# The first gate's logits with stationary weights on four column groups

## The chip, the cores and the metric

The program runs on one core of one Trainium2 chip. Its time is the device time of one execution in microseconds (us), as a median of several runs. The core has five engines with instruction streams of their own: TensorE (PE in the profile, with its weight loads listed apart as PEld), VectorE (DVE), ScalarE (ACT), GpSimd (POOL) and SyncE (SP), which issues most of the transfers. An engine takes its instructions in the order written; engines wait for one another by semaphores.

## The reference, cut to what matters

The kernel computes an attention with a sliding window, then a mixture of experts with a capacity (here called the first one), then a second, dense mixture of experts. The change lies in the gate of the first mixture, whose input x has 1152 rows of 512 features:

```python
logits = x @ w_gate                          # (1152, 512) @ (512, 8)
expert_idx = np.argmax(logits, axis=1)
logits_s = logits - logits.max(-1, keepdims=True)
probs = np.exp(logits_s)
probs /= probs.sum(-1, keepdims=True) + 1e-09
gate_w = probs[np.arange(N), expert_idx]
...                                          # each expert takes its first 288 rows: relu(x w1) w2
out[i] = gate_w[i] * y[expert_idx[i], pos[i]]
```

All of it is computed in fp32, or in pairs of rounded parts that add up to fp32.

## The kernel before, in words

The attention and the first gate form the first stage, which ends some 108 us after the start. The sequence is cut into ten blocks of query rows: two batches of four blocks with 128 rows and one with 64 (block 4 and block 9). The eight heads are done in two groups of four, so there are twenty units; unit u belongs to block u // 2. For a unit the steps are `scores` (PE; operands on 64 partitions, two heads side by side on the two halves of the array's rows), `pick` and `limit` (DVE), `powers` (ACT), `turn_p` (PE transposes), `take_p` (the transposed powers into SBUF, on ACT, DVE and POOL), `values` (PE) and `norm` (DVE).

When both units of a block t are done, the gate follows: `turn_x.t` (four PE transposes), `take_x.t` (ACT copies them into `xT`), `logits.t` (PE), `top.t` (DVE finds the largest logit and its index), `gate.t` (ACT, the exponentials), `choice.t`, `count.t`, `place.t`, `mark.t`, `table.t`, `add_table.t` (DVE and PE, the row's place in its expert's list) and `scale_x.t` (the scaled row goes to DRAM).

The order of all steps is written out by hand in the string `ORDER`. A step name that stands there several times is a generator that goes on one piece at each place (`top.0` stands three times, for its three pieces). After each step the helper `in_order` ties every new instruction to the one before it on its engine, so each engine's stream is the order of that string. An engine does not skip an instruction that waits.

`logits` holds a 128x128 part of `xT` stationary and streams the gate's eight weight columns, repeated 15 times to 120 columns. There are four such matmuls, one for each 128 features, and they accumulate into one PSUM tile `lgp`. An fp32 matmul appears in the trace as two records, called passes here, so a block has eight. PSUM tiles with the tag "pt" come from one pool of four buffers: `lgp` and the transposes share it.

After the first stage come the eight experts of the first mixture (up to about 264 us), then the second mixture with PE busy nearly without a break to the end.

Of the kernel before, what the change touches and what calls it, by code (L numbers as in the profile page):

```python
# [33 lines left out]
rest_k.2 limit.2.0 turn_k.4 norm.0 take_k.4 limit.2.1 limit.2.1 powers.1.1 norm.0 turn_p.1.1 powers.2.0 scores.3
turn_p.2.0 rest_k.4 norm.0 turn_k.3 turn_q.3 pick.3.0 limit.3.0 limit.3.0 scores.4 load_v.1 powers.2.1 take_p.1.0
take_k.3 values.1.0 load_weight.1 pick.3.1 take_p.2.0 take_p.1.1 powers.3.0 limit.3.1 rest_k.3 turn_p.2.1 limit.3.1
split_hi.0 split_lo.0 split_hi.1 split_hi.2 values.1.1 split_hi.3 turn_q.4 pick.4.0 limit.4.0 split_lo.1 turn_p.3.0
split_lo.2 split_lo.3 limit.4.0 powers.4.0 norm.1 norm.1 scores.5 norm.1 take_p.2.1 pick.4.1 values.2.1 pick.5.1
take_p.3.0 load_weight.2 load_v.2 take_q.3 turn_x.0 limit.5.1 take_q.4 limit.4.1 rest_q.3 powers.3.1 load_block.5
take_x.0 values.2.0 load_weight.3 split_hi.4 limit.4.1 turn_p.3.1 norm.2 limit.5.1 split_lo.4 split_hi.5 pick.5.0  # L40
split_lo.5 norm.2 logits.0 split_hi.6 take_p.3.1 split_hi.7 turn_p.4.0 scores.6 top.0 norm.2 powers.5.1 limit.5.0
top.0 values.3.0 limit.5.0 pick.6.1 rest_q.4 take_p.4.0 split_hi.8 limit.6.1 pick.6.0 turn_p.5.1 values.3.1
limit.6.1 top.0 powers.4.1 norm.3 split_lo.6 turn_p.4.1 load_block.6 split_hi.9 split_hi.10 norm.3 scores.7
limit.6.0 split_hi.11 turn_k.5 norm.3 values.4.0 take_p.5.1 powers.5.0 turn_p.5.0 choice.0 pick.7.0 take_p.4.1
pick.7.1 limit.6.0 split_lo.7 values.4.1 limit.7.1 turn_q.5 gate.0 powers.6.1 take_p.5.0 turn_p.6.1 limit.7.1 norm.4
take_k.5 powers.6.0 take_q.5 scores.8 choice.0 norm.4 norm.4 turn_x.1 pick.8.0 take_p.6.1 limit.8.0 limit.7.0
limit.7.0 take_x.1 values.5.1 turn_p.6.0 load_v.3 values.5.0 turn_k.6 rows pick.8.1 limit.8.0 norm.5 logits.1
rest_k.5 take_k.6 top.1 count.0 norm.5 powers.7.0 take_p.6.0 norm.5 scores.9 pick.9.0 rest_k.6 powers.8.0 turn_x.2
# [3 lines left out]
powers.9.1 scale_x.0 turn_q.7 limit.10.1 powers.8.1 norm.6 choice.1 place.1 scores.11 top.2 norm.6 values.7.1  # L52
limit.11.0 take_p.7.0 powers.9.0 top.2 powers.10.0 take_q.7 turn_p.8.0 limit.11.1 limit.11.0 gate.2 load_block.9
rest_q.7 turn_p.8.1 turn_k.7 take_p.8.1 take_k.7 top.2 values.7.0 norm.7 norm.7 scale_x.1 load_v.8 take_p.8.0
turn_p.9.0 turn_p.9.1 norm.7 turn_p.10.0 take_p.9.0 scores.12 powers.10.1 turn_x.3 values.8.1 values.8.0 turn_p.10.1
choice.2 take_p.9.1 take_x.3 pick.12.1 logits.3 limit.12.1 rest_k.7 mark.0 norm.8 norm.8 limit.11.1 norm.8 count.2
take_p.10.0 pick.12.0 top.3 top.3 limit.12.1 limit.12.0 table.0 add_table.0 values.9.0 place.2 values.9.1
powers.11.1 take_p.10.1 norm.9 choice.2 limit.12.0 top.3 turn_p.11.1 powers.11.0 scores.13 take_p.11.1 norm.9 norm.9
values.10.0 load_block.8 turn_x.4 turn_p.11.0 mark.1 take_x.4 choice.2 choice.3 pick.13.0 gate.3 take_p.11.0
powers.12.1 values.10.1 load_v.6 pick.13.1 limit.13.0 table.1 logits.4 limit.13.0 norm.10 limit.13.1 count.3  # L60
add_table.1 scale_x.2 turn_k.8 norm.10 norm.10 turn_p.12.1 powers.12.0 split_lo.8 limit.13.1 values.11.1 turn_p.12.0
values.11.0 place.3 take_k.8 norm.11 turn_q.8 mark.2 scores.14 norm.11 top.4 norm.11 take_p.12.0 take_p.12.1
choice.3 powers.13.0 powers.13.1 rest_k.8 pick.14.0 top.4 limit.14.0 choice.3 gate.4 take_q.8 values.12.0 load_v.7
pick.14.1 table.2 limit.14.0 turn_p.13.1 top.4 values.12.1 mark.3 scale_x.3 powers.14.0 turn_q.9 rest_q.8 norm.12
turn_p.13.0 add_table.2 scores.15 norm.12 take_p.13.0 norm.12 take_p.13.1 turn_x.5 choice.4 take_x.5 values.13.0
turn_p.14.0 values.13.1 limit.14.1 take_q.9 limit.14.1 pick.15.0 pick.15.1 logits.5 rest_q.9 limit.15.1 limit.15.0
take_p.14.0 count.4 powers.14.1 table.3 turn_p.14.1 norm.13 limit.15.1 powers.15.1 top.5 norm.13 scores.16 choice.4
place.4 top.5 norm.13 take_p.14.1 limit.15.0 choice.3 gate.5 top.5 choice.4 pick.16.0 turn_p.15.1 scale_x.4
pick.16.1 take_p.15.1 values.14.1 turn_x.6 choice.5 limit.16.0 mark.4 values.14.0 load_v.9 turn_k.9 powers.15.0
limit.16.0 limit.16.1 choice.5 take_x.6 powers.16.0 choice.1 limit.16.1 turn_p.15.0 scores.17 norm.14 add_table.3  # L70
choice.5 take_k.9 norm.14 logits.6 count.5 take_p.15.0 norm.14 pick.17.1 pick.17.0 powers.16.1 top.6 turn_p.16.0
choice.5 top.6 place.5 values.15.0 rest_k.9 turn_p.16.1 values.15.1 limit.17.1 top.6 limit.17.0 choice.6 limit.17.1
table.4 gate.6 choice.6 limit.17.0 count.6 take_p.16.0 norm.15 choice.6 norm.15 scores.18 norm.15 choice.6
powers.17.0 place.6 scale_x.6 scale_x.5 mark.5 take_p.16.1 pick.18.1 mark.6 values.16.0 turn_p.17.0 limit.18.1
limit.18.1 values.16.1 pick.18.0 powers.17.1 add_table.4 table.5 norm.16 ids add_table.5 table.6 norm.16 scores.19
take_p.17.0 powers.18.1 turn_p.17.1 norm.16 limit.18.0 add_table.6 limit.18.0 pick.19.0 powers.18.0 first_window
values.17.0 pick.19.1 take_p.17.1 limit.19.1 turn_p.18.0 take_p.18.0 limit.19.1 turn_x.7 limit.19.0 take_x.7
values.17.1 turn_p.18.1 limit.19.0 powers.19.0 norm.17 logits.7 norm.17 turn_p.19.0 norm.17 take_p.18.1 powers.19.1
split_lo.9 turn_x.8 top.7 values.18.0 take_p.19.0 top.7 values.18.1 norm.18 take_x.8 choice.4 top.7 norm.18 choice.0
turn_p.19.1 logits.8 norm.18 choice.2 take_p.19.1 gate.7 top.8 values.19.0 choice.7 choice.7 top.8 choice.7  # L80
values.19.1 norm.19 norm.19 first_turn.1 top.8 norm.19 choice.7 count.7 gate.8 turn_x.9 first_turn.0 take_x.9
choice.8 place.7 logits.9 mark.7 choice.8 choice.8 top.9 table.7 count.8 first_add.7.0 top.9 choice.8 top.9 gate.9
place.8 first_add.7.1 choice.9 count.9 choice.9 first_add.8.1 choice.9 choice.9 scale_x.7 place.9 first_add.8.0
first_add.9.1 scale_x.9 split_lo.10 scale_x.8 mark.9 first_add.9.0 mark.8 table.9 first_split.1 first_split.0
table.8 split_lo.11 add_table.7 add_table.8 load_weight.5 add_table.9
# [1394 lines left out]
```

## Time and profile before

| what | value |
|---|---|
| median of 3 runs | 1038.63 us (1038.39 to 1039.27) |
| the profiled execution's own time | 1038.18 us |
| span from its first to its last instruction | 1036.1 us |
| PE busy | 1018.7 us, 98% of the span |
| PE weight loads (PEld) busy | 930.3 us, 90% |
| DVE busy | 677.8 us, 65% |
| ACT busy | 387.3 us, 37% |
| POOL busy | 315.5 us, 30% |

The shares are averages over stages with different limits. The change lies in the first tenth of the span alone, so that stage has to be read by itself. A busy time of PE counts pipelined matmuls from their start to their modelled end, so it says that work was in flight and not how dense it was. In a row of the timeline the columns are start, duration of the merged group, engine, line, operation, tile written and tiles read, shapes and the count of instructions.

### The profile page before, as it was taken

How to read it: one execution, taken by the hardware profiler on the slowest of the kernel's cores; microseconds unless marked ns; L12 is line 12 of the kernel's file. 1: busy time of each engine (PE TensorE's matmuls, PEld its weight loads, DVE VectorE, ACT ScalarE, POOL GpSimd, SP SyncE). 2: the span in 40 equal slices, each digit the busy share in tenths (PEclk: the TensorE clock that was granted, in tenths of full speed). 3: DMA queues.
4: the chain of work that ended last, by engine and by line, in shares of the span. 5: the costliest groups of instructions: out<-in, count | busy, mean ns of one | idle time of the engine just before them, and what ended most of it. 6: DMA issues, size and time to landing. Idle time of an engine off the chain costs nothing.

```text
span 1036.1 us, 16836 instructions
## 1 busy us (share of the span) xinstructions
PE 1018.7 (98%) x6388; PEld 930.3 (90%) x6388; DVE 677.8 (65%) x1644; ACT 387.3 (37%) x838; POOL 315.5 (30%) x305
## 2 busy tenths in 40 slices
PE   8999999999999999999999999999999999999997
PEld 6888999999889998999898999999898999999896
DVE  7988788778783347575756657575756657575752
ACT  6744477767321313232332323232322323232320
POOL 6533153341200123341313332241313332242113
PEclk9999999999999999999999999999999999999999
DMA  9931589986200112020211112020211112020102
...
DMA packets 74103, 83.22 MB, mean 80 GB/s; under 512 B 31585, under 2 KB 45921, under 8 KB 74018
## 3 DMA queue, kind: packets, MB, share of 16 engines
...
q14 instruction: 34, 0.28, 0.1%
...
## 4 chain that ended last, share of the span: by engine, by line
PE 72%; issue 2%; POOL 1%; DVE 1%; POOLq 0%; ACT 0%
PE pr L1414 31%; PE pr L1383 30%; PE ops L1340 5%; PE hps L1301 5%; PE pb L772 1%; POOL out_dram L1418 1%; PE pb L776 1%; PE lps L1074 0%; DVE tsums L1187 0%; POOL w_wlo L1278 0%; PE cps L1111 0%; POOLq L1476 0%; DVE lsb L1078 0%; DVE y_lo L1184 0%; PE ltp L1081 0%
## 5 line engine op out<-in xcount | busy, mean ns | idle before, releaser
L1414 PE MATMUL pr<-w_whi,hT 128*128 128x512 f32 x1008 | 315.8, 390 | 0.2 <-DVE hT L1375 0.2
L1414 PEld LDWEIGHTS pr<-w_whi,hT 128*128 128x128 f32 x1008 | 189.2, 188 | 39.5 <-DVE hT L1375 0.5
L1414 PE MATMUL pr<-w_wlo,hT 128*128 128x512 f32 x504 | 196.4, 390 | 0.0
L1278 POOL TENSOR_TENSOR w_wlo<-r,w_whi 128x512 fp32r<-128x512 f32 x56 | 71.4, 1294 | 290.4 <-ACT w_whi L1277 180.5
L1416 DVE SCALAR_TENSOR_TENSOR acc<-pr,Pm,acc 128x512 f32<-128x512 f32 x126 | 91.3, 745 | 89.0 <-PE pr L1414 88.7
L1374 ACT ACTIVATE hT<-pr 128x256 fp32r<-128x256 f32 (+1 forms) x168 | 69.0, 411 | 176.0 <-DVE pr L1391 176.0
L1375 DVE SCALAR_TENSOR_TENSOR hT<-pr,hT 128x256 fp32r<-128x256 f32 (+1 forms) x168 | 77.0, 458 | 80.1 <-ACT hT L1374 80.1
L1383 PE MATMUL pr<-y_hi,wy 128*128 128x320 f32 (+1 forms) x560 | 122.7, 297 | 0.0
L1414 PEld LDWEIGHTS pr<-w_wlo,hT 128*128 128x128 f32 x504 | 94.6, 188 | 19.5 <-POOL w_wlo L1278 0.5
L1383 PEld LDWEIGHTS pr<-y_hi,wy 128*128 128x128 f32 x560 | 93.8, 188 | 0.3 <-DVE hT L1375 0.3
L1271 POOL TENSOR_TENSOR wy<-r,wy 128x512 fp32r<-128x512 f32 x28 | 40.0, 1427 | 172.1 <-ACT wy L1270 172.1
L1383 PE MATMUL pr<-y_lo,wy 128*128 128x256 f32 (+1 forms) x280 | 83.3, 297 | 0.0
L191 DVE TENSOR_TENSOR wlo<-w,whi 128x1024 fp32r<-128x1024 f32 x66 | 80.7, 1225 | 3.1 <-issue 3.1
L179 ACT CAST whi<-w 128x1024 fp32r<-128x1024 f32 x66 | 69.1, 1051 | 19.5 <-DMA w<-in_moe_w_dram 15.3
L772 PE MATMUL pb<-h,whi 128*128 128x384 f32 x256 | 74.9, 361 | 0.4 <-DVE t L792 0.4
L772 PE MATMUL pb<-xt,whi 128*128 128x384 f32 x256 | 74.3, 362 | 0.6 <-PEq L946 0.3
L1277 ACT CAST w_whi<-r 128x512 fp32r<-128x512 f32 x56 | 33.1, 619 | 94.1 <-PE pr L1414 93.2
L1374 ACT ACTIVATE hT<-h 128x256 fp32r<-128x256 f32 (+1 forms) x56 | 24.9, 445 | 115.7 <-DVE h L1391 115.7
L1383 PE MATMUL pr<-y_hi,wx_wlo 128*128 128x256 f32 (+1 forms) x224 | 64.6, 288 | 0.0
L1383 PE MATMUL pr<-y_hi,wx_whi 128*128 128x256 f32 (+1 forms) x224 | 64.4, 288 | 0.0
L1383 PE MATMUL pr<-y_lo,wx_whi 128*128 128x256 f32 (+1 forms) x224 | 64.4, 287 | 0.0
L1255 POOL TENSOR_TENSOR sums<-r 128x512 f32<-128x512 f32 x28 | 37.0, 1324 | 80.8 <-DMA r<-in_moe_w_dram 45.6
...
## 6 DMA issues: line engine op xcount, KB each, us to landing
...
```

The costliest lines, as they stand in the source:

```text
L179: nc.scalar.copy(his[i][:, sl, :], raws[i][:, sl, :])
L191: nc.vector.tensor_tensor(out=los[i][:, sl, :], in0=raws[i][:, sl, :], in1=his[i][:, sl, :].bitcast(F32), op=ALU.subtract)
L772: nc.tensor.matmul(ps[:, 0:2 * W], whi, x.rearrange("p r w -> p (r w)"), start=(m == 0), stop=(m == K - 1))
L1271: nc.gpsimd.tensor_tensor(out=wy[1][:, i], in0=x, in1=wy[0][:, i].bitcast(F32), op=ALU.subtract)
L1278: nc.gpsimd.tensor_tensor(out=w2p[1][:, k], in0=x, in1=w2p[0][:, k].bitcast(F32), op=ALU.subtract)
L1301: nc.tensor.matmul(hpss[f], a, bb[c][:, cols], start=(c == 0 and m == 0), stop=(c == ND - 1 and m == 2))
L1340: nc.tensor.matmul(ops, a[:, tcol], bb, start=(m == 0), stop=(m == 3 * NF - 1))
L1374: nc.scalar.activation(hi, src, AF.Relu)
L1375: nc.vector.scalar_tensor_tensor(out=lo, in0=src, scalar=0.0, in1=hi.bitcast(F32), op0=ALU.max, op1=ALU.subtract)
L1383: nc.tensor.matmul(ps, a[:, i, c, f], b, start=(c == 0 and m == 0), stop=(c == 1 and m == 2))
L1414: nc.tensor.matmul(ops, a[:, k, s * P:(s + 1) * P], b[:, k, :], start=(m == 0), stop=(m == 6 * QP - 1))
L1416: nc.vector.scalar_tensor_tensor(out=acc[s], in0=ops, scalar=Pm[:, s, e:e + 1], in1=acc[s], op0=ALU.mult, op1=ALU.add)
```

## The change

`logits(t)` is exchanged for blocks 0 to 7. The weights become stationary: for each of the four parts of the features a tile of 128 rows and 32 columns (eight weights and 24 zeros) is loaded into its own group of 32 columns of the array, and the block's rows of `xT` (128 columns, or 64 in block 4) stream through it. The four results lie below one another in PSUM, on partitions 0, 32, 64 and 96. ACT copies them to a new SBUF tile `lgs`. A new step `add_logits(t)`, one fp32 matmul with `lgs` stationary and a matrix `sel` of ones and zeros streaming, adds the four and puts rows back onto partitions. `top` then reads that. Blocks 8 and 9 keep the old form.

In `ORDER`, `add_logits.t` stands right before `top.t` for all eight blocks: behind `scores.6`, `scores.9`, `scores.11`, `table.0`, `scores.14`, `turn_p.14.1`, `turn_p.16.0` and `turn_x.8`. `top.1` and `top.3` move back with it, and `turn_p.16.0` stands one place earlier against `top.6`. No other step moves.

`wg1_sb` grows from 8 to 32 columns for each part and is cleared on POOL before its transfer; `sel` comes from one DVE reduction of the identity.

```diff
         def zero_row(_):
+            nc.gpsimd.memset(wg1_sb, 0.0)
+            nc.vector.tensor_reduce(out=sel, in_=ident.rearrange("p (c e) -> p e c", e=32)[:, 0:E, :], op=ALU.add, axis=AX.X)
             nc.sync.dma_start(out=wg2_sb, in_=wg2.rearrange("(c p) e -> p c e", p=P))
-            nc.sync.dma_start(out=wg1_sb, in_=wg1.rearrange("(c p) e -> p c e", p=P))
+            nc.sync.dma_start(out=wg1_sb[:, :, 0:E], in_=wg1.rearrange("(c p) e -> p c e", p=P))
...
         def logits(t):
             n = blocks[t][2]
             lgp = ps_t.tile([P, ND * P], F32, tag="pt", name="lgp")
+            if t < NT - 2:
+
+                for c in range(ND):
+                    nc.tensor.matmul(lgp[32 * c:32 * c + 32, 0:n], wg1_sb[:, c, :], gt['xT', t][:, c, :n],
+                                     start=True, stop=True, tile_position=(0, 32 * c))
+                lgs = wk.tile([P, P], F32, tag="lgs", name="lgs", bufs=1)
+                nc.scalar.copy(lgs[:, :n], lgp[:, :n])
+                gt['lgs', t] = (lgp, lgs)
+                return
             for c in range(ND):
 
-                nc.tensor.matmul(lgp[:n, 0:15 * E], gt['xT', t][:, c, :n], wg1_sb[:, c:c + 1, :].to_broadcast([P, 15, E]),
+                nc.tensor.matmul(lgp[:n, 0:15 * E], gt['xT', t][:, c, :n], wg1_sb[:, c:c + 1, 0:E].to_broadcast([P, 15, E]),
                                  start=(c == 0), stop=(c == ND - 1))
             gt['lg', t] = lgp
+
+        def add_logits(t):
+
+            n = blocks[t][2]
+            lgp, lgs = gt['lgs', t]
+            nc.tensor.matmul(lgp[:n, P:P + 15 * E], lgs[:, :n], sel[:, None, :].to_broadcast([P, 15, E]), start=True, stop=True)
+            gt['lg', t] = lgp[:, P:P + E]
```

## Rows read from the trace of the kernel before

**Rows 1.** The page's first line.
```profile
span 1036.1 us, 16836 instructions
```
**Rows 2.** Stretches of 10 us: start:end, length, then busy us (count) of each engine.
```profile
20.00:30.00 10.00, 9.20 (x82) 7.88 (x81) 8.12 (x42) 9.33 (x24) 8.80 (x10) 1.00 0.97 281
...
50.00:60.00 10.00, 9.47 (x81) 7.55 (x79) 8.10 (x48) 4.38 (x13) 2.35 (x5) 1.00 0.52 105
...
70.00:80.00 10.00, 9.63 (x95) 8.42 (x93) 9.92 (x63) 5.15 (x16) 2.55 (x4) 1.00 0.14 43
...
90.00:100.00 10.00, 9.78 (x69) 8.05 (x69) 7.27 (x46) 3.60 (x12) 4.36 (x5) 1.00 0.13 41
```
**Rows 3.** Timeline around the logits of block 0: start, us, engine, line.
```profile
23.09 1.06 PE L532 MATMUL xps<-vb,pT 128*128 128x128 f32 x8
...
25.57 0.97 PEld L583 LDWEIGHTS lgp<-wg_sb,xT 128*128 128x128 f32 x8 [0.34 <-ACT xT L575]
25.57 1.15 PE L583 MATMUL lgp<-wg_sb,xT 128*128 128x120 f32 x8
...
26.76 0.17 DVE L595 MAX8 m<-lgp 128x8 f32<-128x8 f32 x1
...
26.87 0.98 PE L444 MATMUL sps<-kS,qT 64*128 64x256 f32 x12
```
**Rows 4.** PE groups by form (0 to 140 us): count, busy us, mean ns.
```profile
L532 PE MATMUL xps<-vb,pT 128*128 128x128 f32 x196 | 28.4, 281 | 2.0 <-DVE pT L506 0.6 <-DVE x L561 0.6 <-PE sps L444 0.5
...
L522 PE MATMUL xps<-vb,pT 64*128 64x130 f32 x16 | 3.9, 322 | 0.0
```
**Rows 5.** Timeline: mixed rows, side by side, and 64 stationary columns.
```profile
11.04 0.72 PE L437 MATMUL sps<-kF,qF 64*128 64x128 f32 x8
...
93.97 1.75 PE L522 MATMUL xps<-vb,pT 128*128 128x130 f32 x8
...
101.41 0.81 PEld L583 LDWEIGHTS lgp<-wg_sb,xT 128*64 128x64 f32 x8
```
**Rows 6.** ACT groups by form (0 to 108 us), the smallest copy out of PSUM.
```profile
L508 ACT COPY pT<-ptp 128x128 f32<-128x128 f32 x4 | 1.1, 265 | 2.8 <-PE ptp L488 1.7 <-DVE pT L506 1.1
```
**Rows 7.** Timeline around the logits of block 5.
```profile
72.86 0.38 ACT L508 COPY pT<-ptp 128x256 f32<-128x256 f32 x1 [0.83 <-PE ptp L488]
...
73.13 1.05 ACT L479 ACTIVATE pr<-sc,nmx 128x128 f32<-128x128 f32 x3
...
73.44 1.10 PE L583 MATMUL lgp<-wg_sb,xT 128*128 128x120 f32 x8
...
74.58 0.17 DVE L595 MAX8 m<-lgp 128x8 f32<-128x8 f32 x1
...
74.97 0.42 PE L488 MATMUL ptp<-ident,pr 128*128 128x128 f32 x2
```
**Rows 8.** Timeline: scores and largest logit in block 4.
```profile
64.84 0.98 PE L444 MATMUL sps<-kS,qT 64*128 64x256 f32 x12
...
65.42 0.14 DVE L595 MAX8 m<-lgp 64x8 f32<-64x8 f32 x1
```
**Rows 9.** Timeline around the logits of block 6.
```profile
79.67 0.38 ACT L508 COPY pT<-ptp 128x256 f32<-128x256 f32 x1 [0.42 <-PE ptp L488]
...
80.47 1.15 PE L583 MATMUL lgp<-wg_sb,xT 128*128 128x120 f32 x8
```
**Rows 10.** Waits before 110 us: who for whom, us, times, longest.
```profile
DVE pT L506 <- ACT pT L508: 1.6, 1, 1.6
```
**Rows 11.** Timeline of SP and POOL at the step zero_row.
```profile
13.59 0.58 SPq L328 DMA_DIRECT2D wg_sb<-in_moe_w_gate_dram  x1
...
14.63 1.27 POOL L394 TENSOR_TENSOR kS<-raw,kS 128x512 fp32r<-128x512 f32 x1
```
**Rows 12.** Stretches of 1 us behind the first stage; the granted clock stands after POOL.
```profile
111.00:112.00 1.00, 1.00 (x5) 1.00 (x5) 0.00 (x0) 0.00 (x0) 0.69 (x2) 0.50 0.92 352
...
114.00:115.00 1.00, 1.00 (x9) 1.00 (x8) 1.00 (x2) 0.28 (x1) 0.00 (x0) 1.00 0.76 209
```

More of the change, by code (lines that the diff above doesn't have):

```diff
@@ L34 @@
[L34 to L48, printed above, removed]
+take_q.0 load_block.2 scores.0 load_v.0 limit.0.1 turn_q.1 load_block.4 constants take_k.1 take_q.1 rest_k.1 limit.0.0
@@ new lines @@
+turn_k.2 turn_q.2 load_block.3 limit.0.1 load_weight.0 limit.0.0 more_constants powers.0.1 rest_q.1 powers.0.0
+scores.1 turn_p.0.1 turn_p.0.0 take_k.2 limit.1.0 take_q.2 limit.1.0 scores.2 take_p.0.0 limit.1.1 sides rest_q.2
+zero_row powers.1.0 take_p.0.1 limit.1.1 pick.2.0 pick.2.1 values.0.0 turn_p.1.0 limit.2.0 values.0.1 rest_k.2
+limit.2.0 turn_k.4 norm.0 take_k.4 limit.2.1 limit.2.1 powers.1.1 norm.0 turn_p.1.1 powers.2.0 scores.3 turn_p.2.0
+rest_k.4 norm.0 turn_k.3 turn_q.3 pick.3.0 limit.3.0 limit.3.0 scores.4 load_v.1 powers.2.1 take_p.1.0 take_k.3
@@ new lines @@
+values.1.0 load_weight.1 pick.3.1 take_p.2.0 take_p.1.1 powers.3.0 limit.3.1 rest_k.3 turn_p.2.1 limit.3.1 split_hi.0
+split_lo.0 split_hi.1 split_hi.2 values.1.1 split_hi.3 turn_q.4 pick.4.0 limit.4.0 split_lo.1 turn_p.3.0 split_lo.2
+split_lo.3 limit.4.0 powers.4.0 norm.1 norm.1 scores.5 norm.1 take_p.2.1 pick.4.1 values.2.1 pick.5.1 take_p.3.0
+load_weight.2 load_v.2 take_q.3 turn_x.0 limit.5.1 take_q.4 limit.4.1 rest_q.3 powers.3.1 load_block.5 take_x.0
+values.2.0 load_weight.3 split_hi.4 limit.4.1 turn_p.3.1 norm.2 limit.5.1 split_lo.4 split_hi.5 pick.5.0 split_lo.5
@@ new lines @@
+norm.2 logits.0 split_hi.6 take_p.3.1 split_hi.7 turn_p.4.0 scores.6 add_logits.0 top.0 norm.2 powers.5.1 limit.5.0
+top.0 values.3.0 limit.5.0 pick.6.1 rest_q.4 take_p.4.0 split_hi.8 limit.6.1 pick.6.0 turn_p.5.1 values.3.1 limit.6.1
+top.0 powers.4.1 norm.3 split_lo.6 turn_p.4.1 load_block.6 split_hi.9 split_hi.10 norm.3 scores.7 limit.6.0
+split_hi.11 turn_k.5 norm.3 values.4.0 take_p.5.1 powers.5.0 turn_p.5.0 choice.0 pick.7.0 take_p.4.1 pick.7.1
+limit.6.0 split_lo.7 values.4.1 limit.7.1 turn_q.5 gate.0 powers.6.1 take_p.5.0 turn_p.6.1 limit.7.1 norm.4 take_k.5
@@ L49 @@
+powers.6.0 take_q.5 scores.8 choice.0 norm.4 norm.4 turn_x.1 pick.8.0 take_p.6.1 limit.8.0 limit.7.0 limit.7.0
+take_x.1 values.5.1 turn_p.6.0 load_v.3 values.5.0 turn_k.6 rows pick.8.1 limit.8.0 norm.5 logits.1 rest_k.5 take_k.6
+count.0 norm.5 powers.7.0 take_p.6.0 norm.5 scores.9 add_logits.1 top.1 pick.9.0 rest_k.6 powers.8.0 turn_x.2
 values.6.0 pick.9.1 limit.9.0 limit.8.1 load_block.7 turn_q.6 place.0 limit.9.1 powers.7.1 choice.0 top.1 turn_p.7.1
@@ L51 @@
 take_p.7.1 logits.2 load_weight.4 norm.6 choice.1 load_v.5 limit.10.0 limit.10.0 load_v.4 count.1 limit.10.1
[L52 to L85, printed above, removed]
+powers.9.1 scale_x.0 turn_q.7 limit.10.1 powers.8.1 norm.6 choice.1 place.1 scores.11 add_logits.2 top.2 norm.6
@@ new lines @@
+values.7.1 limit.11.0 take_p.7.0 powers.9.0 top.2 powers.10.0 take_q.7 turn_p.8.0 limit.11.1 limit.11.0 gate.2
+load_block.9 rest_q.7 turn_p.8.1 turn_k.7 take_p.8.1 take_k.7 top.2 values.7.0 norm.7 norm.7 scale_x.1 load_v.8
+take_p.8.0 turn_p.9.0 turn_p.9.1 norm.7 turn_p.10.0 take_p.9.0 scores.12 powers.10.1 turn_x.3 values.8.1 values.8.0
+turn_p.10.1 choice.2 take_p.9.1 take_x.3 pick.12.1 logits.3 limit.12.1 rest_k.7 mark.0 norm.8 norm.8 limit.11.1 norm.8
+count.2 take_p.10.0 pick.12.0 limit.12.1 limit.12.0 table.0 add_logits.3 top.3 top.3 add_table.0 values.9.0 place.2
@@ new lines @@
+values.9.1 powers.11.1 take_p.10.1 norm.9 choice.2 limit.12.0 top.3 turn_p.11.1 powers.11.0 scores.13 take_p.11.1
+norm.9 norm.9 values.10.0 load_block.8 turn_x.4 turn_p.11.0 mark.1 take_x.4 choice.2 choice.3 pick.13.0 gate.3
+take_p.11.0 powers.12.1 values.10.1 load_v.6 pick.13.1 limit.13.0 table.1 logits.4 limit.13.0 norm.10 limit.13.1
+count.3 add_table.1 scale_x.2 turn_k.8 norm.10 norm.10 turn_p.12.1 powers.12.0 split_lo.8 limit.13.1 values.11.1
+turn_p.12.0 values.11.0 place.3 take_k.8 norm.11 turn_q.8 mark.2 scores.14 norm.11 add_logits.4 top.4 norm.11
@@ new lines @@
+take_p.12.0 take_p.12.1 choice.3 powers.13.0 powers.13.1 rest_k.8 pick.14.0 top.4 limit.14.0 choice.3 gate.4 take_q.8
+values.12.0 load_v.7 pick.14.1 table.2 limit.14.0 turn_p.13.1 top.4 values.12.1 mark.3 scale_x.3 powers.14.0 turn_q.9
+rest_q.8 norm.12 turn_p.13.0 add_table.2 scores.15 norm.12 take_p.13.0 norm.12 take_p.13.1 turn_x.5 choice.4 take_x.5
+values.13.0 turn_p.14.0 values.13.1 limit.14.1 take_q.9 limit.14.1 pick.15.0 pick.15.1 logits.5 rest_q.9 limit.15.1
+limit.15.0 take_p.14.0 count.4 powers.14.1 table.3 turn_p.14.1 norm.13 limit.15.1 powers.15.1 add_logits.5 top.5
@@ new lines @@
+norm.13 scores.16 choice.4 place.4 top.5 norm.13 take_p.14.1 limit.15.0 choice.3 gate.5 top.5 choice.4 pick.16.0
+turn_p.15.1 scale_x.4 pick.16.1 take_p.15.1 values.14.1 turn_x.6 choice.5 limit.16.0 mark.4 values.14.0 load_v.9
+turn_k.9 powers.15.0 limit.16.0 limit.16.1 choice.5 take_x.6 powers.16.0 choice.1 limit.16.1 turn_p.15.0 scores.17
+norm.14 add_table.3 choice.5 take_k.9 norm.14 logits.6 count.5 take_p.15.0 norm.14 pick.17.1 pick.17.0 powers.16.1
+turn_p.16.0 add_logits.6 top.6 choice.5 top.6 place.5 values.15.0 rest_k.9 turn_p.16.1 values.15.1 limit.17.1 top.6
@@ new lines @@
+limit.17.0 choice.6 limit.17.1 table.4 gate.6 choice.6 limit.17.0 count.6 take_p.16.0 norm.15 choice.6 norm.15
+scores.18 norm.15 choice.6 powers.17.0 place.6 scale_x.6 scale_x.5 mark.5 take_p.16.1 pick.18.1 mark.6 values.16.0
+turn_p.17.0 limit.18.1 limit.18.1 values.16.1 pick.18.0 powers.17.1 add_table.4 table.5 norm.16 ids add_table.5
+table.6 norm.16 scores.19 take_p.17.0 powers.18.1 turn_p.17.1 norm.16 limit.18.0 add_table.6 limit.18.0 pick.19.0
+powers.18.0 first_window values.17.0 pick.19.1 take_p.17.1 limit.19.1 turn_p.18.0 take_p.18.0 limit.19.1 turn_x.7
@@ new lines @@
+limit.19.0 take_x.7 values.17.1 turn_p.18.1 limit.19.0 powers.19.0 norm.17 logits.7 norm.17 turn_p.19.0 norm.17
+take_p.18.1 powers.19.1 split_lo.9 turn_x.8 add_logits.7 top.7 values.18.0 take_p.19.0 top.7 values.18.1 norm.18
+take_x.8 choice.4 top.7 norm.18 choice.0 turn_p.19.1 logits.8 norm.18 choice.2 take_p.19.1 gate.7 top.8 values.19.0
+choice.7 choice.7 top.8 choice.7 values.19.1 norm.19 norm.19 first_turn.1 top.8 norm.19 choice.7 count.7 gate.8
+turn_x.9 first_turn.0 take_x.9 choice.8 place.7 logits.9 mark.7 choice.8 choice.8 top.9 table.7 count.8 first_add.7.0
@@ L722, in fused_kernel @@
             turn_k, take_k, rest_k, turn_q, take_q, rest_q, scores, pick, limit, powers, turn_p, take_p, values, norm,
[L723 removed]
+            turn_x, take_x, logits, add_logits, top, gate, choice, scale_x, count, place, mark, table, add_table, clear_windows,
             first_window, first_turn, first_add, first_split, split_hi, split_lo)}
```

11 lines of the change are left out of this document (5 added, 6 removed).

## The prediction

> **What bounds the kernel now.** The profiled execution took 1038.18 us: a span of 1036.1 [rows 1] and 2.1 around it. It lies 0.45 below the median of 1038.63, so the sum is made on 1038.18 and 0.45 is added at its end. A difference of 0.2%, 2.1 us, is about what a measurement here can tell from none; "faster", "same" and "slower" mean that bound.
>
> I read first the busy time by stretches of 10 us, because the change lies in the first stage alone. There PE and DVE are both nearly full, and it changes which of them leads [rows 2]. From 20 to 30 us ACT has 9.33 of 10 and DVE 8.12. From 70 to 80 DVE has 9.92: nothing that holds DVE up there can be made good. From 50 to 60 (the short block 4) DVE idles 1.9, and from 90 to 100 (the short block 9) 2.7. PE counts 9.2 to 9.8 everywhere, but that is work in flight, so its density has to come from the timeline.
>
> Second, the timeline around one block's gate [rows 3]. Eight fp32 passes (128 stationary columns, 120 streaming) load in 0.97, or 0.12 each, and the largest logit is sought on DVE at 26.76, right behind them. What stands after the first stage runs on a PE that is busy nearly throughout, so a shift of the stage's end should pass one to one into the span.
>
> **The change part by part.**
>
> *The passes.* Removed: eight passes of 0.12, 0.97 a block. The same eight come back with 32 columns to load and 128 to stream. Two rows bound them. With 64 columns to load instead of 128, the short block's eight loads still take 0.81 [rows 5], 0.10 each: the stream sets the pace once the load is short. So one after another, eight passes cost 0.8. But matmuls on separate halves of the rows do run side by side: L437 puts eight passes of 128 columns into 0.72, against 1.06 for L532's eight on the whole array [rows 3, 5]. Less the 0.28 that a single matmul of such a kind lasts [rows 4], that is 0.44 against 0.78, about half. No row has separate column groups. Four groups side by side would be two rounds, 0.2, and the first round pays its load too, 0.3 in all. I take 0.3, because the row halves are the nearest thing, and keep 0.8 as the other end.
>
> The Trainium skill has the rule for this: "TensorEngine Tiling (Array Packing)", section Performance Considerations, advises for a streaming side of at most 32 columns to swap it with the stationary one and use four column tiles. By its overview that is up to four times as fast; 0.97 would become 0.24. That agrees with my lower end, and leaves out the next term.
>
> *The mode changes.* L522's eight passes alternate between 128 and 64 rows of operands after every two [rows 4], and take 1.75 where L532's eight of nearly the same columns take 1.06 [rows 3, 5]. Three changes inside cost 0.69, so 0.2 each: the array has to run empty. The new passes use the array in a third way, so they pay 0.2 on entering and 0.2 on leaving. In blocks 2 and 6 `scores` (64 rows) stands right ahead, and a change was paid there already: one is new. In block 7 64-row transposes stand on both sides: none is new. So 2+2+1+2+2+2+1+0 = 12 changes, 2.4 us. The bound below is nothing, if a drain of 32 columns costs nothing.
>
> *The adding matmul.* Two passes of 0.12, 0.24 a block.
>
> *PE's sum.* Eight blocks: before 8 x 0.97 = 7.8. After 8 x (0.3 + 0.24) + 2.4 = 6.7. PE gains 1.1. With free changes it gains 3.5; with passes one after another it loses 8 x 0.5 - 1.1 = 2.9.
>
> *The copy on ACT.* 128x128 out of PSUM, 0.27 [rows 6], eight times 2.1 us. ACT has that time after 50 us [rows 2]. Its place matters more: the copy stands right behind `logits` in ACT's stream, so ACT, which used to run ahead of PE, now stands until PE has finished. In block 5, ACT did `take_p.14.0` at 72.86 and `powers.14.1` from 73.13, while PE only began the logits at 73.44 [rows 7]. Now both stand behind a copy that can start at about 73.44 + 0.2 + 0.3 + 0.28 = 74.2 and ends at 74.5; then 0.38 for the copy and 0.7 for two of the exponentials give 75.6. `turn_p.14.1` (PE, 74.97) needs them: PE stands 0.6. In block 6 `take_p.15.0` was copied at 79.67 and the logits begin at 80.47 [rows 9]: the new copy ends at 81.4, so `take_p.15.0` is 1.7 late. DVE's half of that step has waited for ACT's half before [rows 10], so DVE may stand as long. I take half, 0.85.
>
> *The largest logit.* It now waits for scores or a transpose on PE, then the adding matmul; behind it on DVE are `norm`, `limit` and `take_p`, for which `values` and `powers` wait. Block 0: the logits save 0.97 - 0.3 - 0.4 = 0.27, so `turn_p.4.0` and the scores end their issue at 27.85 - 0.28 - 0.27 = 27.3 [rows 3]; then a change, two passes and 0.28 to land give 28.0, where DVE was ready at 26.76. DVE stands 1.25. Block 4: issue of the scores ends at about 65.82 - 0.28 = 65.5, so the result is there at 66.1 instead of 65.42 [rows 8]: 0.7. Block 5: `turn_p.14.1` at 75.6, then 0.25 for its two transposes, two passes and 0.28: 76.3 instead of 74.58 [rows 7], 1.7. Blocks 1 and 3 have `top` moved back, and block 7's falls where DVE idles 2.7 of 10 [rows 2]: nothing. Block 2, with scores in between as in block 4, I leave out; at block 4's rate it would be 0.7 more.
>
> Added up, DVE stands 1.25 in block 0, 0.7 in block 4, 1.7 in block 5, 0.85 in block 6. The first is covered by the 1.9 that DVE idles from 50 to 60 us; if that idle time were PE's fault and moved along, it would cost 1.25 more. The other three, 3.25, fall where DVE has hardly any idle time. Of them I let the second half of PE's gain (0.55) and some of the idle time at the end (0.4) give back 0.95, leaving 2.3.
>
> *Setup.* The reduction for `sel` on DVE is small; between nothing and the 1.27 of a POOL instruction on 128x512 I take 0.2. The clearing on POOL goes ahead of the subtraction at 14.63, so the transfer of the weights, 13.59 before, moves to about 14.9 [rows 11]; SP's queue stands 1.3 there, and behind it are the zero row, the values of block 1 and the next expert weights. The DMA engines are still full from 20 us on, with a share of 0.97 [rows 2], so I take nothing; without that cover up to 1.3.
>
> Sum: 2.3 + 0.2 = 2.5. 1038.18 + 2.5 = 1040.7, and with 0.45: **1041.2 us**, +0.25%.
>
> **The rivals.**
>
> *PE leads and gains.* If the waits fall into idle time as a whole, PE's 1.1 to 3.5 comes through: 1035.1 to 1037.5, faster from a gain of 2.1 on, which needs mode changes of 0.1 or less. For it speaks that PE is never below 9.2 in these rows; against it 70 to 80 us, where DVE has 9.92. Chance 0.15.
>
> *Nothing to measure.* PE's gain and DVE's stands cancel within 2.1: 1036.6 to 1040.7. For it: the stage has been tight on two engines, and each gives a little. 0.31.
>
> *The groups don't run side by side.* Then the change does not do what it says: PE loses 2.9 instead of gaining 1.1, and every wait grows by 0.5 a block; 1041.2 + 3 = 1044.2. Against it L437's 0.72. 0.10. The skill has a rule that would lead there: "TensorE: Matmul & The Clock Gate", section Part 3, says that weight loads pass under running matmuls only where the row groups differ, and here all four groups use all rows. The trace does not bear it out for whole-array matmuls: the eight loads of L583 take 0.97 beside matmuls of the same rows that take 1.15 [rows 3].
>
> *A clock stretch more, or one less.* Behind the first stage the granted clock fell to 0.50, the 1.2 GHz level, and a microsecond held 5 matmuls instead of 9 [rows 12]; some 3 us of it cost 1.3. It came right behind the stage's thin end, which the new passes make thinner. A second such stretch adds 1.3: 1042.5. Chance 0.08.
>
> **How the numbers follow.** My forecast (1040.8 to 1043) has 0.36. Faster is the first rival, 0.15; same is the second, 0.31; slower is the forecast, serial groups and the clock, 0.54. Eight in ten lie between 1037.2 and 1044.6: below are the larger gains of PE, above a serial array with little hidden. For the likeliest case alone: 1040.0 to 1043.0.
>
> **What would show it.** In the profile of the changed kernel: the eight passes of a block in about 0.6 with the last one's landing (1.2 if serial), and some 0.2 missing before and after; DVE idle for 3 to 5 us before the largest logits, most in blocks 0 and 5; ACT waiting for the logits; the stage's end, the first `pb` matmul, 2 to 3 us later. The forecast is wrong if DVE's stands are made good before block 5, if transposes or scores come early enough that `add_logits` finds DVE still at work, or if the clock stretch moves.

## The result and the profile after

The changed kernel takes 1048.31 us (median of 4 runs, 1047.23 to 1049.22); the kernel before, beside it, 1038.95 (4 runs, 1038.39 to 1039.58). The ratio is 1.0096 [1.0079, 1.0113]: slower by 9.4 us where 2.5 were forecast. The profiled execution took 1047.71 us. Two later executions of the kernel before, of 2817 and 3486 us, stand far outside the rest and enter no number here. The page's first line, which answers to [rows 1]:

```profile
span 1046.0 us, 16882 instructions
```

The span is 9.9 us longer. Two marks split it. The first matmul of the experts (`pb`) starts at 108.61 us in the trace of before and at 115.13 here, from the two timelines:

```profile
108.61 0.45 PE L772 MATMUL pb<-xt,whi 128*128 128x384 f32 x1 [0.25 <-DVE xt L237]
```
```profile
115.13 0.45 PE L792 MATMUL pb<-xt,whi 128*128 128x384 f32 x1 [0.25 <-DVE xt L237]
```

So the first stage ends 6.5 us later. That understates what the change costs, because this execution came to the gate earlier. Ahead of block 0's logits only the setup differs, and yet they start at 25.57 us in the trace of before [rows 3] and at 24.34 here. With one and the same kernel that start varies too; a second execution of the kernel before (e8, below) has these rows:

```profile
24.89 1.15 PE L583 MATMUL lgp<-wg_sb,xT 128*128 128x120 f32 x8
...
108.03 0.45 PE L772 MATMUL pb<-xt,whi 128*128 128x384 f32 x1 [0.25 <-DVE xt L237]
```

From block 0's logits to the end of the stage the kernel before takes 83.04 and 83.14 us, and the changed kernel 90.79. Counted from there the first stage is 7.7 us longer.

The second mixture's first matmul (`hps`) starts at 264.00 before and at 273.24 after: between the marks 155.4 us became 158.1, another 2.7. Behind the second mark 0.7 is left.

The logits in the timeline, which answer to [rows 3] (block 0):

```profile
24.34 0.16 PEld L588 LDWEIGHTS lgp<-xT,wg_sb 128*32 128x32 f32 x8 [0.17 <-issue]
...
24.34 0.43 PE L588 MATMUL lgp<-xT,wg_sb 128*32 128x128 f32 x8
24.70 0.44 PE L492 MATMUL ptp<-ident,pr 128*128 128x128 f32 x2
...
25.98 0.48 PE L604 MATMUL lgp<-sel,lgs 128*128 128x120 f32 x2
```

Eight passes take 0.43 us with the last one's landing, where they took 1.15, and the next step starts 0.36 behind their start instead of 0.99. The column groups run side by side. Stretches of 10 us, which answer to [rows 2]; the number after POOL's is the granted clock:

```profile
20.00:30.00 10.00, 9.32 (x93) 7.93 (x94) 8.78 (x49) 9.55 (x25) 10.00 (x11) 1.00 1.07 298
...
50.00:60.00 10.00, 9.21 (x74) 7.02 (x72) 6.86 (x36) 4.17 (x13) 2.36 (x5) 0.90 0.46 105
60.00:70.00 10.00, 10.00 (x72) 8.65 (x73) 6.65 (x34) 3.86 (x15) 1.75 (x2) 0.59 0.32 80
70.00:80.00 10.00, 8.92 (x95) 7.51 (x92) 8.45 (x43) 4.28 (x15) 3.25 (x6) 1.00 0.08 29
```

Two things are new. DVE, 9.92 busy from 70 to 80 us before, has 8.45, though not in the same work: block 5's logits start at 73.44 before and at 78.69 here. And TensorE's clock, 1.00 throughout the first 100 us before, is 0.90 and 0.59 from 50 to 70. The waits from 20 to 116 us (who <- for whom: us in total, times, longest) name the engine that stands:

```profile
ACT lgs L591 <- PE lgp L588: 9.5, 6, 2.3
...
DVE pT L510 <- ACT pT L512: 3.7, 3, 1.8
...
DVE m L615 <- PE lgp L604: 2.7, 4, 0.8
...
PE lgp L662 <- ACT raw L397: 1.4, 1, 1.4
...
PE tab L685 <- ACT raw L397: 0.8, 1, 0.8
```

ACT stands 9.5 us for the logits, since the copy is next in its stream. The last two rows are what follows: PE waits for a copy of ACT (`raw`, the step `rest_k`) that stands behind the logits' copy and empties one of the four "pt" buffers, for which the next `count` (L662) or `table` (L685) waits. Block 3 in the timeline:

```profile
56.22 0.27 ACT L591 COPY lgs<-lgp 128x128 f32<-128x128 f32 x1 [1.65 <-PE lgp L588]
56.39 0.59 ACT L397 COPY raw<-pt 128x512 f32<-128x512 f32 x1
...
55.68 0.42 PE L588 MATMUL lgp<-xT,wg_sb 128*32 128x128 f32 x8
56.03 0.18 PE L662 MATMUL lgp<-oh,tri 128*128 128x8 bf16 x1
...
57.03 0.17 PE L685 MATMUL tab<-zero_b,ones_b 128*96 128x24 bf16 x1 [0.79 <-ACT raw L397]
```

PE begins the logits at 55.68, ACT has stood 1.65 us when its copy begins, `rest_k.7` follows at 56.39, and `table.0` on PE stands 0.79 for it. In the trace of before the table starts 0.06 behind `count.2`:

```profile
55.45 0.17 PE L642 MATMUL lgp<-oh,tri 128*128 128x8 bf16 x1
...
55.51 0.19 PE L665 MATMUL tab<-zero_b,ones_b 128*96 128x24 bf16 x1
```

Stretches of 1 us of the changed kernel behind that place:

```profile
56.00:57.00 1.00, 0.24 (x6) 0.17 (x3) 0.96 (x5) 0.78 (x3) 0.00 (x0) 1.00 0.06 8
...
58.00:59.00 1.00, 1.00 (x4) 0.77 (x4) 0.53 (x7) 0.69 (x3) 0.33 (x1) 0.51 0.00 0
...
67.00:68.00 1.00, 1.00 (x7) 1.00 (x6) 1.00 (x6) 0.38 (x2) 0.00 (x0) 0.50 0.00 0
68.00:69.00 1.00, 1.00 (x10) 1.00 (x10) 0.41 (x1) 0.16 (x1) 0.00 (x0) 0.87 0.00 0
```

PE is busy 0.24 of the microsecond from 56, and from 58 to 68 the clock is granted at 0.50, the 1.2 GHz level. Block 1 has the same wait with no fall of the clock behind it; its rows are in the next section but one.

### The profile page after: what moved, and what is told of

Same layout as the page of the kernel before. It is cut to its first block, busy times and chain, and to the rows that moved or that the text cites. A ratio compares the mean times of both kernels' runs of the same rounds, so it can differ in the third digit from the quotient of the medians.

```text
span 1046.0 us, 16882 instructions
## 1 busy us (share of the span) xinstructions
PE 1021.8 (98%) x6404; PEld 929.8 (89%) x6404; DVE 675.8 (65%) x1645; ACT 388.3 (37%) x846; POOL 319.2 (31%) x306
## 4 chain that ended last, share of the span: by engine, by line
PE 71%; issue 2%; DVE 1%; POOL 1%; POOLq 0%; ACT 0%
PE pr L1434 31%; PE pr L1403 29%; PE ops L1360 5%; PE hps L1321 4%; PE pb L792 1%; POOL out_dram L1438 1%; PE pb L796 1%; DVE tsums L1207 0%; PE lps L1094 0%; POOL w_wlo L1298 0%; DVE y_lo L1204 0%; PE cps L1131 0%; POOLq L1496 0%; DVE lsb L1098 0%; DVE h_lo L1332 0%
```

## The experiments

They ran in four groups, e1 to e4, e5 to e8, e9 to e11 and e12 to e14, each beside the kernel before, on three chips by the record (6, 4, 4 and 8). There the kernel before spread from 1034.7 to 1044.9 us, with medians of 1039.6 to 1040.2, so small ratios have wide intervals.

The first stage can be read more finely, from one execution of each kernel. Its end, the first `pb` matmul, is called the mark below. Where block 0's logits start varies from 24.10 to 26.08 us among all traces and carries through to the mark. Counted from that start, the seven traces with the old logits agree within 0.1 us, so the column "logits.0 to mark" is the one that tells the kernels apart.

| kernel | ratio to before | logits.0, us | mark, us | logits.0 to mark, us | marks apart, us |
|---|---|---|---|---|---|
| before, first profile | | 25.57 | 108.61 | 83.04 | 155.4 |
| before, again (e8) | 0.9985 [0.9968, 1.0002] | 24.89 | 108.03 | 83.14 | 154.9 |
| the change | 1.0096 [1.0079, 1.0113] | 24.34 | 115.13 | 90.79 | 158.1 |
| e1 all copies late | 1.0035 [1.0010, 1.0059] | 24.98 | 108.21 | 83.23 | 155.7 |
| e2 old passes, new waits | 1.0097 [1.0063, 1.0131] | 25.11 | 115.98 | 90.87 | 158.2 |
| e4 filler in `count.2` | 1.0084 [1.0058, 1.0110] | 26.08 | 114.31 | 88.23 | 160.0 |
| e5 only block 3's copy late | 1.0060 [1.0037, 1.0083] | 25.22 | 112.08 | 86.86 | 156.7 |
| e7 only block 3's copy early | 1.0053 [1.0035, 1.0071] | 24.10 | 111.14 | 87.04 | 157.9 |
| e6 tuned | 1.0002 [0.9983, 1.0021] | 24.96 | 107.78 | 82.82 | 160.7 |
| e14 tuned, again | 1.0018 [0.9997, 1.0039] | 25.32 | 108.18 | 82.86 | 156.6 |
| e11 tuned, cleared early | 1.0017 [1.0000, 1.0035] | 24.28 | 106.99 | 82.71 | 157.3 |
| e3 setup alone | 1.0023 [1.0001, 1.0045] | 24.80 | 107.89 | 83.09 | 161.4 |
| e13 setup alone, again | 1.0014 [0.9992, 1.0035] | 25.06 | 108.14 | 83.08 | 155.5 |
| e9 wide tile alone | 1.0006 [0.9987, 1.0024] | 25.35 | 108.41 | 83.06 | 155.3 |
| e10 clearing alone | 0.9981 [0.9968, 0.9994] | 25.24 | 108.31 | 83.07 | 154.7 |
| e12 sel alone | 1.0001 [0.9982, 1.0020] | 25.57 | 108.64 | 83.07 | 158.4 |

**e1: the copy's place.** The copy to `lgs` moves from the end of `logits` into `add_logits`; nothing else changes.

```diff
 def logits(t):
-    lgs = wk.tile(...); nc.scalar.copy(lgs[:, :n], lgp[:, :n])
 def add_logits(t):
+    lgs = wk.tile(...); nc.scalar.copy(lgs[:, :n], lgp[:, :n])
     nc.tensor.matmul(lgp[:n, P:P + 15 * E], lgs[:, :n], sel..., start=True, stop=True)
```

> ACT's copy of the four partial logits moves from the step logits to the step add_logits, behind the ACT steps that stand between. Theory A (the copy's place in ACT's stream holds ACT up, so a PSUM buffer and exponentials come late, PE idles and the clock falls): 4 to 6 us of the 9.4 come back, 1042 to 1044, and the low clock around 58 to 68 us is gone. Theory B (the forecast: DVE stands for the largest logit behind add_logits): the time stays within 1.5 of the changed kernel's 1048.3, since add_logits comes no earlier.

The first stage gives back nearly all it had lost: it takes 83.23 us from block 0's logits to the mark, 0.1 to 0.2 more than before, and the low clock is gone. The time, 1042.41, lies in the range of theory A. Start and mark, and the same waits as shown for the changed kernel:

```profile
24.98 0.43 PE L588 MATMUL lgp<-xT,wg_sb 128*32 128x128 f32 x8
...
108.21 0.44 PE L792 MATMUL pb<-xt,whi 128*128 128x384 f32 x1 [0.25 <-DVE xt L237]
```
```profile
DVE m L615 <- PE lgp L604: 3.6, 3, 1.7
...
PE xps L536 <- DVE x L565: 2.0, 3, 0.7
...
ACT lgs L603 <- PE lgp L588: 1.3, 3, 0.5
```

ACT's stand falls from 9.5 us to 1.3, and the copy's place costs 7.6 (90.79 - 83.23). Column groups and changes of the array's form are all still in e1, so the loss does not come from them. DVE's stand for the largest logit grows from 2.7 to 3.6, and PE waits 2.0 us for `norm` on DVE (`x`, which frees what `values` write), where it waited 0.6 before [rows 4] and 2.1 in the changed kernel; for the late copies themselves it waits 1.0. Yet the stage is hardly longer than before: these waits seem to take from PE about what the column passes give it.

**e2: the old passes with the new waits.** The eight passes are those of the kernel before, on the whole array; the copy on ACT and the adding matmul (with the identity in place of `lgs`, two passes as well) stay at their places.

```diff
-nc.tensor.matmul(lgp[32 * c:32 * c + 32, 0:n], wg1_sb[:, c, :], gt['xT', t][:, c, :n], ...)
+nc.tensor.matmul(lgp[:n, 0:15 * E], gt['xT', t][:, c, :n], wg1_sb[:, c:c + 1, 0:E].to_broadcast([P, 15, E]), ...)
```

> The changed kernel with the old eight passes on the whole array, but still the copy on ACT at the same place and an adding matmul (with the identity) at the same place: same waits, no changes of the array's mode. Theory C (the mode changes are what costs): 12 x 0.2 = 2.4 us and more come back, 1044 to 1046. Theory A: the passes take 0.7 longer a block, ACT is held as much longer, so no better than the changed kernel: 1048 to 1053.

From block 0's logits to the mark it takes 90.87 us, where the changed kernel has 90.79, and the time, 1049.8, is what theory A expected. So the new waits alone, with no column groups and no changes of form, cost as much. That the two agree so closely is chance. The longer passes hold ACT longer, and on the other side the clock does not fall: behind the same stand in block 3 it stays at 1.00.

```profile
59.25 0.17 PE L685 MATMUL tab<-zero_b,ones_b 128*96 128x24 bf16 x1 [0.86 <-ACT raw L397]
```
```profile
60.00:70.00 10.00, 9.48 (x88) 7.77 (x86) 7.47 (x42) 5.62 (x20) 2.42 (x4) 1.00 0.32 80
```

**e5 and e7: block 3's copy, both ways.** A step `copy_logits` takes the copy out of `logits`, so that `ORDER` places it. In e5 seven copies stay where the change put them:

```diff
-... logits.3 limit.12.1 rest_k.7 mark.0 ...               (the copy inside logits.3)
+... logits.3 limit.12.1 rest_k.7 copy_logits.3 mark.0 ...
```

> Only one copy is moved: block 3's, from ahead of rest_k.7 to behind it on ACT; the other seven stand where the change put them. Theory (the copy held rest_k.7, which frees the buffer that table.0 needs; PE stood 0.8 us and ran at clock 0.50 from 58 to 68 us): no low clock there, table.0 no longer shifted against logits.3, and of the changed kernel's 9.4 us some 3 to 4 are gone, 1044 to 1045 us. Rival (the low clock comes from the column passes or from the thinner work as a whole): the stretch from 58 to 68 stays at 0.50 and the time at 1048.

In e7 all are late, as in e1, but block 3's copy stands ahead of `rest_k.7`.

> The counterpart: the kernel with all copies moved late, but block 3's alone stands where the change put it, ahead of rest_k.7. Theory: PE stands some 0.8 us ahead of table.0, the clock falls to 0.50 behind it, and the first stage is 3 to 4 us longer than with all copies late: 1045 to 1046.5 us. Rival (it needs the delays of the other blocks too): no low clock, within 1 us of all copies late, 1042.4.

The timelines of e5, then e7 (`copy_logits.3`, `rest_k.7` and the first matmul of `table.0`):

```profile
55.27 0.59 ACT L398 COPY raw<-pt 128x512 f32<-128x512 f32 x1
...
56.90 0.19 PE L691 MATMUL tab<-zero_b,ones_b 128*96 128x24 bf16 x1
...
57.02 0.27 ACT L603 COPY lgs<-lgp 128x128 f32<-128x128 f32 x1 [1.16 <-PE lgp L589]
```
```profile
54.44 0.27 ACT L603 COPY lgs<-lgp 128x128 f32<-128x128 f32 x1 [1.65 <-PE lgp L589]
54.60 0.59 ACT L398 COPY raw<-pt 128x512 f32<-128x512 f32 x1
...
55.25 0.17 PE L691 MATMUL tab<-zero_b,ones_b 128*96 128x24 bf16 x1 [0.79 <-ACT raw L398]
```

And a stretch of 1 us behind it, again e5 and then e7:

```profile
58.00:59.00 1.00, 1.00 (x7) 0.64 (x5) 0.97 (x12) 1.00 (x4) 0.00 (x0) 1.00 0.00 0
```
```profile
60.00:61.00 1.00, 1.00 (x7) 0.69 (x5) 1.00 (x5) 0.00 (x0) 0.92 (x1) 0.50 0.09 16
```

With the copy late the table does not wait and the clock stays at 1.00; with it early, the same 0.79 of stand and the clock at 0.50 from 58 to 65 us. From block 0's logits to the mark the difference is 90.79 - 86.86 = 3.9 one way and 87.04 - 83.23 = 3.8 the other: one copy of 0.27 us costs nearly 4 us at this place. The other seven together cost 86.86 - 83.23 = 3.6. e7's time fell into the expected range. e5's, 1046.84, is above it, but the kernel before took 1040.17 beside it, where the range counted from 1038.95; by the ratios (1.0096 and 1.0060) 3.7 us came back, as expected.

**e4: filling the thin place.** Eight passes of the old kind, whose result nobody reads, are put into `count.2`, so PE has work while it would stand.

> The changed kernel with eight more fp32 passes whose result nobody reads, on PE right behind the logits of block 3, where PE otherwise idles 0.8 us for a PSUM buffer. Theory A (that idle time lets the clock fall, and the low clock costs 3 us): the clock stays up from 58 to 68 us and the time falls to 1044 to 1046, although PE has more to do. Rival (the clock falls for some other reason, or costs little): 1048 to 1050.

The first row is the stretch with the filler, the second one 14 us earlier:

```profile
58.00:60.00 2.00, 2.00 (x26) 1.57 (x25) 1.71 (x9) 1.03 (x4) 0.20 (x1) 1.00 0.56 88
```
```profile
44.00:45.00 1.00, 1.00 (x6) 1.00 (x5) 1.00 (x10) 0.97 (x3) 0.91 (x4) 0.50 1.28 252
```

The clock stays up behind block 3, as it should by the theory of the stand. But in this execution it fell near 43 us, behind block 1, for some 3 us, and the time, 1049.07, went as the rival expected. The price of the clock can still be read, from the start of block 3's logits to the start of block 4's: 6.96 us before, 10.34 in the changed kernel and 7.56 here, with the filler's 1.0 in it. e7 takes 9.09, e2 with its stand and no fall 8.08, e1 and e5 6.86. The filler takes up PE about as long as it stood, so 10.34 - 7.56 = 2.8 us is about what the low clock costs in that stretch; e2, whose passes are longer, sets 2.3 beside it. Of the nearly 4 us that the copy costs in block 3, the low clock is thus the larger part and the stand itself the smaller.

**e6, e14, e11: the version meant to be best.** Block 0's copy stays right behind its logits, the others are late; block 5's goes ahead of `powers.15.1`; block 4's adding matmul goes ahead of `scores.14`; in blocks 0 and 5 DVE's ready work goes ahead of `top`. e14 is the same kernel again; e11 clears the weights' tile at the start on POOL.

```diff
-... mark.2 scores.14 norm.11 add_logits.4 top.4 ...       (the copy inside logits.4)
+... mark.2 copy_logits.4 add_logits.4 scores.14 norm.11 top.4 ...
-... powers.15.1 add_logits.5 top.5 norm.13 scores.16 choice.4 place.4 ...
+... copy_logits.5 powers.15.1 add_logits.5 norm.13 choice.4 place.4 top.5 scores.16 ...
```

> The version meant to be best: column passes in all eight blocks; block 0's copy right behind its logits, the others late; block 5's copy ahead of powers.15.1; block 4's adding matmul ahead of scores.14; in blocks 0 and 5 what DVE has ready stands ahead of the largest logit. If PE's saving is worth what it saves once no engine stands for it, the first stage is 1 to 2 us shorter than before and the time 1037 to 1038 us beside a kernel before of 1038.6 to 1040. If DVE's work sets the stage's pace, it is no shorter than with all copies late (0.4 us shorter than before) and the time is within 0.2% of before.

> The tuned kernel (clearing at zero_row) once more. Its first stage should take 107.0 to 107.8 us again. If the setup as a whole lengthens the experts' stage: 158 or more between the marks (160.7 the first time) and a time at or above before. If it was the spread of single executions: 155 to 157 and a time of 1037 to 1039.

> The tuned kernel, with the clearing of the weights' tile at the very start on POOL, so that SP's queue does not stand for it. If the held queue costs the 2 to 7 us that the setup runs lost behind the first stage: SP's issue of the gate's weights follows its neighbour at once, experts' stage 155 to 156, time 1037 to 1039. If not: experts' stage spreads as before (157 to 161), time as the tuned kernel's, 1040.

From block 0's logits to the mark they take 82.82, 82.86 and 82.71 us, where the kernel before has 83.04 and 83.14: the stage is 0.2 to 0.4 us shorter. (e11's early mark, 106.99, is owed to its early start, 24.28.) That is less than the 1 to 2 us hoped for. The times are 1.0002, 1.0018 and 1.0017 of before, so no version beats it, and the early clearing, for which 1037 to 1039 was expected, gave 1040.87.

**What lies behind the first stage.** The changed kernel lost 2.7 us between the marks, where no instruction differs. e8 is the kernel before; e3 has the setup alone (32-column tile, clearing, `sel`; old logits), e9, e10 and e12 one part each.

```diff
+nc.gpsimd.memset(wg1_sb, 0.0)                             # e3; e10: four times, narrow tile
+nc.vector.tensor_reduce(out=sel, in_=ident..., ...)        # e3, e12
-wg1_sb = ac.tile([P, ND, E], F32, name="wg1_sb")
+wg1_sb = ac.tile([P, ND, 32], F32, name="wg1_sb")          # e3, e9
```

> The kernel before with only the change's setup: the weights' tile of 32 columns cleared on POOL ahead of its transfer, and the reduction for sel. Forecast: 0.2 us, so 1038.7 to 1039.3. Rival (SP's queue held behind the clearing starves block 1's values and the next weights): up to 1.3 us, 1040.3.

> The kernel before, unchanged, with a profile. Its experts' stage (first expert matmul to the second mixture's) took 155.4 us in the first profile and 155.7 to 161.4 in the experiments. If the runs of one program spread as much, its time from the same two marks differs from 155.4 by more than 2 us here; if each program has its own, it stays within 1 us of 155.4.

> The kernel before with one thing more: the tile of the gate's weights is 32 columns wide for each quarter of the features and is loaded in its first 8; nothing is cleared, no sel, old logits. If the wider tile (where the later tiles lie in SBUF, how the load is written) is what lengthens the experts' stage: from its first expert matmul to the second mixture's 158 us or more instead of 155, time 1041 to 1043. If it is the held queue: 155 to 156 and the time of before.

> The kernel before with one thing more: four clearings on POOL of the gate's weights' tile ahead of its load, so that SP's queue stands as in the changed kernel (some 1.4 us, and the expert weights behind it come later); the tile stays 8 wide, old logits. If the held queue lengthens the experts' stage: 158 us or more between its marks and 1041 to 1043 in time. If it is the tile: 155 to 156 and the time of before.

> The kernel before with one thing more: the tile sel and its reduction on DVE at the place of zero_row; narrow tile of the weights, nothing cleared. If this part lengthens the experts' stage: 158 us or more between the marks, time 2 to 4 us above before. If not: 155 to 156 and within 0.2% of before.

> The setup alone, once more (wider tile, clearing, sel; old logits), the same kernel as in the earlier run of it. If the setup as a whole lengthens the experts' stage: again 158 us or more between the marks (161.4 the first time), ratio at 1.002 or above with an interval that excludes 1. If the first was the spread of single executions: 155 to 157, ratio around 1.000.

e8 stayed within 1 us of 155.4 (154.9), which would fit a length of each program's own. The second mark in e3 and in e13, the same kernel, speaks against that:

```profile
269.25 0.33 PE L1304 MATMUL hps<-y_hi,whi 128*128 128x384 f32 x1
```
```profile
263.69 0.33 PE L1304 MATMUL hps<-y_hi,whi 128*128 128x384 f32 x1
```

One program took 161.4 us between the marks in one execution and 155.5 in another; so did the tuned one (160.7 and 156.6). The two executions of each ran on different chips, but e13's twelve, on one chip, spread from 1037.3 to 1046.6 as well. So the 158.1 of a single profile is by itself no evidence that the change costs anything there. In e3 most of the difference is one stand:

```profile
199.03 1.04 ACT L179 CAST whi<-w 128x1024 fp32r<-128x1024 f32 x1 [4.14 <-DMA w<-in_moe_w_dram]
...
201.61 0.63 PE L775 MATMUL pb<-h,whi 128*128 128x384 f32 x1 [4.05 <-DVE t L795]
```

ACT waits 4.14 us for a transfer of expert weights, and behind that cast come its copy out of PSUM, the sum `t` on DVE, and PE. Why that transfer came late was not tried. Neither the wide tile nor the held queue (SP waiting for the clearing) lengthens the stage (155.3, 154.7); `sel` alone had 158.4 with a time of 1.0001.

The times leave something open all the same. Both runs of the setup and three of the four with the copies late (e1, e6, e14, e11) lie 0.14 to 0.35% above before with a first stage that is hardly longer. The change, e2, e4, e5 and e7 lie 9.4, 10.1, 8.7, 6.2 and 5.5 us above before, 1.5 to 3.6 us more than their first stages lose in the traces. So about 2 us of the change's 9.4 may go with its setup, though none of the three parts shows it alone. At 0.2%, that is at the edge of what these runs can tell, and its cause was not found.

## Why the prediction was wrong

**The step that failed is "The copy on ACT".** It said that the copy's place matters more than its 0.27 us and followed it in blocks 5 and 6. Where it looked, it was near: at block 5 it had PE standing 0.6 for the exponentials, and the trace shows 0.70; at block 6 it took 0.85, and there PE stands 1.04 and DVE 1.18:

```profile
80.38 0.41 PE L492 MATMUL ptp<-ident,pr 128*128 128x128 f32 x2 [0.70 <-ACT pr L483]
...
87.71 0.42 DVE L510 TENSOR_TENSOR pT<-ptp,side 128x256 f32<-128x256 f32 x1 [1.18 <-ACT pT L512]
...
88.19 0.44 PE L492 MATMUL ptp<-ident,pr 128*128 128x128 f32 x2 [1.04 <-DVE pT L510]
```

It did not look at blocks 1 and 3, because `top.1` and `top.3` had moved back and "The largest logit" put both at nothing. But ACT's copy is not behind `top`; it is behind `logits`, and in these two blocks a `rest_k` stands next in ACT's stream. Block 1 (PE, then ACT):

```profile
38.17 0.42 PE L588 MATMUL lgp<-xT,wg_sb 128*32 128x128 f32 x8
40.01 0.17 PE L662 MATMUL lgp<-oh,tri 128*128 128x8 bf16 x1 [1.42 <-ACT raw L397]
```
```profile
38.72 0.27 ACT L591 COPY lgs<-lgp 128x128 f32<-128x128 f32 x1 [2.34 <-PE lgp L588]
38.88 0.59 ACT L395 CAST kS<-pt 128x512 fp32r<-128x512 f32 x1
39.36 0.61 ACT L397 COPY raw<-pt 128x512 f32<-128x512 f32 x1
```

ACT stands 2.34 us, `rest_k.5` ends at 39.97, and PE stands 1.42 for its buffer. Measured against the kernel before, `count.0` is 0.96 further behind `logits.1`, and by `logits.2` 1.4 us are lost (7.71 from one to the other, 6.35 before). With block 3's 3.9 that is 5.3, against the 5.2 by which the first stage exceeds the forecast (7.7 against 2.5). From the start of one block's logits to the next the changed kernel loses 0.38, 1.36, 0.61, 3.38, 0.75, 0.87 and 0.97 us (blocks 0 to 6; part of block 3's low clock falls into block 4), and it gets 0.57 back at the end. The blocks other than 1 and 3 together thus lose 3.0, not far from the forecast's 2.5; block by block its terms were not as near.

The rest of the 9.4 us, 1.7, lies behind the stage, where the forecast had nothing, and stays open.

**The clock rival** named what then showed, a thin place with a fall of the clock behind it, at the wrong place and too small. It was looked for behind the stage's end, at 1.3 us. There the changed kernel has its fall again, from 116 to 119 us; it is no fixture, since e8, the kernel before again, has none. The new one came at block 3, some 10 us long, and with the stand that it follows costs nearly 4 us. The stand was visible in advance: the pool of four buffers and ACT's order are both written in the kernel.

**The largest logit** was mis-sized the other way. DVE's stand was forecast at 3.65 in blocks 0, 4 and 5; the whole wait is 2.7. In e1 it is 3.6, near the forecast, but what it does to the stage together with all of PE's gains and losses comes out at 0.1 to 0.2 us, where the forecast had these terms lose more than a microsecond: that part went as the rival "Nothing to measure" said. (Block 4's 0.7 also leaves out the 0.2 for a change of form that block 0's sum has.) The sum's 2.5 held terms that cancel and lacked the two that were dear.

**The passes** were right: 0.43 with the last landing, where 0.6 was named for side by side and 1.2 for one after another. The rival that the groups run in turn is out. The Trainium skill's "TensorEngine Tiling (Array Packing)", section Overview, gives up to four times for a dimension of at most 32. The trace agrees in part: from the first pass to the next step 0.99 us became 0.36, a factor of 2.75, and the change of the array's form at the end is in it.

**The mode changes** were taken too dear, 0.2 each. In block 3 the step from the transposes to the logits grew from 0.27 to 0.37, and the one from the logits to `count.2` shrank from 0.89 to 0.35, the change back included. So going in costs 0.10, and what going out costs cannot be told from the passes: the two together take 0.35, where the forecast had 0.3 and 0.2. **PE's sum** of 1.1 held nevertheless, by luck, since it had the mode changes too dear and the adding matmul, 0.24, too cheap: 0.54 less, 0.10 more, and 0.30 for the adding matmul make 0.14 a block, an estimated 1.1 if all eight are like block 3. e2 does not tell how much of it arrives, because the changed kernel's clock fell and e2's did not.

**PE leads and gains** was the rival on the other side. e1, e6, e14 and e11 are its test, with nearly all stands for the early copies taken away: the stage is at best 0.2 to 0.4 us shorter (e6, e14, e11), and the time not better. The 2.0 us of e1's waits are where PE's gain seems to go: the next `values` wait for DVE's `norm`, which stands behind the largest logit.

**Setup**: 0.2 was forecast, and nothing shows in the first stage. With the setup alone block 0's logits start at 24.80 and 25.06, no later than before, and 83.09 and 83.08 lie between them and the mark. SP's queue stands 0.9 us for the clearing in the changed kernel and 1.2 with the setup alone (1.3 in the forecast), and that is hidden there.
